# Loading q and k in 1 KB runs with a GpSimd re-layout, and a new set of order offsets, in a threshold-attention and SwiGLU kernel

## The chip, the core and the metric

The kernel runs on one core of a Trainium2 chip. The core has five engines that run side by side and meet only at semaphores: TensorE (PE, with its weight loads shown apart as PEld), VectorE (DVE), ScalarE (ACT), GpSimd (POOL) and SyncE (SP). SP does no arithmetic here; it issues transfers to the core's 16 DMA engines. Each engine works through its own queue strictly in order: an instruction that waits holds everything behind it on that engine.

The metric is the device time of one execution in microseconds (us), median of several runs.

## What is computed

Two stages. The first is an attention in which only scores within `tau` of their row's maximum count; the second is a normalised SwiGLU feed-forward layer on its result.

```python
# q, k, v: (8 batches, 8 heads, 576, 64) f32; tau = 0.02
scores = scale * (q @ k.T)
thresh = max(scores, axis=-1) - tau
scores = where(scores >= thresh, scores, -1e9)
attn = softmax(scores)
x = (attn @ v) -> (4608 tokens, 512)

# x: (4608, 512); w_gate, w_val: (512, 1536); w_out: (1536, 512)
xn = x / sqrt(mean(x * x) + 1e-6) * rms_g
out = (silu(xn @ w_gate) * (xn @ w_val)) @ w_out
```

## The kernel before, in words

**Tiling.** A batch has 576 rows: 512 main rows and 64 tail rows. The main rows are cut into four chunks of 128 (row `4*si + sc` belongs to chunk `sc`), and the tails of two batches make one more chunk, so there are 36 chunks. A step is one chunk with one pair of heads, so there are 4 steps in a chunk and 144 steps in all.

**A step.** PE multiplies q with k into the PSUM tiles `s_ps` (`emit_burst`, L604). DVE copies the scores out, negated and scaled, with a running row minimum `mx` (L637). POOL makes the bias `nth = mx + tau` from it (L678), a tiny instruction. ACT then masks and exponentiates: in the first 16 steps both heads of a pair go through ACT alone (two L689 and one L696); later one head goes through ACT (L689, L693) and the other through an exponential on ACT (L708) with a mask and a product on POOL (L722, L727). The result `wsb` is transposed, in the first 16 steps by PE (L741) and DVE copies (L750), later by a DMA transpose that SP issues (L756). PE multiplies it with v (`emit_av`, L774 and L779), DVE divides by the row sum (L796, L797), and for each chunk ACT and POOL normalise it (L814 to L822) and SP issues another DMA transpose into `xnT` (L826).

**The feed-forward layer** takes 4 chunks at a time (2 in the first two groups). For each of 12 slices of the hidden width PE makes the gate (L880) and the value (L885), ACT a tanh (L894), DVE two products (L897, L902) into `hf`; then PE multiplies with `w_out` (L951; L926 in the last group, which is streamed), a copy goes to `osb` and SP or ACT issues the store.

**Loads of q and k** (`emit_qk`, L310): for each later batch (1 to 7) and each of 4 pairs of heads there are two loads, k and q, of 256 KB. The destination `qkn` has, in one partition, the order chunk, head, element. In HBM one partition's four rows lie together for one head (4 x 64 floats, 1 KB), so the load is cut into runs of one row (64 floats, 256 B). Three `qkn` buffers take turns (`NQK = 3`); a load into one waits on SP until PE has transposed what was in it (L329). The 16 transposes put q and k of a pair into PSUM, and DVE and ACT copy them to `qkt` (L342, L340). Batch 0 has its own loads (`emit_first`): `load_k` L370 and `load_q` L380, into the same `qkn` buffers.

**v and the weights.** v is loaded in runs of 1 KB into the staging buffers `vst` (L524), from which POOL casts it to f16 in the layout that PE wants (L512). The gate and value weights come through three staging buffers (L1016) and are scaled and cast by POOL (L1023), two casts a load; a load waits on SP until the casts of the load three before it are done. `w_out` is loaded and cast by POOL's own DMA queue (L1035).

**Order.** Nothing is ordered by hand. Every piece of work is an `Op` with an engine, a planned cost, a priority (mostly its step number) and dependencies. `order_ops` plays the engines forward with the planned costs; on each engine it picks, among what can start soonest, the smallest priority. `RANK` adds a constant to the priority of each kind of work, by the function that emits it and the inner function that does it. The order that comes out is the fixed order of each engine's queue. On PE the scores of steps from 32 on come in bursts of 1024 columns, 1.78 steps.

Of the kernel before, what the change touches and what calls it, by code (L numbers as in the profile page):

```python
# [11 lines left out]
ALU = mybir.AluOpType  # L12

LAT = dict(PE=200.0, ACT=130.0, DVE=175.0, POOL=20.0, SP=0.0)
SELF = dict(PE=0.0, ACT=125.0, DVE=178.0, POOL=0.0, SP=0.0)
COST = dict(
    s_main=965.0, s_virt=960.0, tr_qk=570.0, tr4=230.0, tr_full=440.0, av_main=300.0, av_virt=370.0, ffn4=215.8, warm=3500.0,
    evac_qk=600.0, evac_qk_act=465.0, evac_half=252.0, evac_kt=330.0, evac_kt_act=252.0, prelu=667.0, exp2=1060.0, exp1=666.0, exp0=590.0,
    mask_d=680.0, mask_g=1810.0, take_g=1360.0, trw=510.0, evac_w=400.0, evac_wp=900.0, rz=210.0, xmul=341.0, sq=612.0, xn=773.0,
    pool_tiny=302.0, pool_mean=944.0, pool_dma=880.0, cast_v=620.0, cast_vt=475.0, cast_w=665.0,  # L20
    sp=420.0, sp_v=600.0, sp_w=600.0, sp_tr=1300.0, sp_qk=680.0, sp_tl=630.0,
)
DMA_NS = dict(qk=1250.0, tl=700.0, v=880.0, vt=350.0, wt=1700.0, xt=800.0, out=800.0, w=820.0, wo=2500.0)
SWITCH = 125.0

RANK = dict(
    ACT={"emit_ffn/ev": 110, "emit_ffn/store": -50, "emit_ffn/tanh": -20, "emit_k_tail/ev": 100, "emit_q_tail/ev": 60, "emit_qk/ev": -40,
        "emit_softmax/ex": 10, "emit_softmax/prelu": 60, "emit_x/sq": -10, "load_k/load": -80, "transposed/ev": 20},
    DVE={"emit_av/half": -120, "emit_burst/ttr": 31, "emit_ffn/ev": 250, "emit_ffn/gate": 90, "emit_ffn/silu": 29, "emit_k_tail/ev": 30, "emit_qk/ev":
        90, "emit_softmax/ev": 180, "setup/<lambda>": -90, "setup/consts": -110, "setup/vconst": 140, "transposed/ev": 80},  # L30
    PE={"emit_av/fn": 1, "emit_burst/fn": -1.1, "emit_ffn/gmm": 5.1, "emit_ffn/omm": 4.4, "emit_ffn/vmm": 0.7, "emit_k_tail/tr": 30, "emit_q_tail/tr":
        -50, "emit_qk/tr": -90, "emit_softmax/tr": -140, "setup/warm": -10, "transposed/tr": -50},
    POOL={"emit_softmax/mask": -60, "emit_softmax/nthr": -20, "emit_softmax/take": -20, "emit_x/mean": -120, "emit_x/norm": -120, "round_/<lambda>":
        -80, "setup/<lambda>": 70, "main/<lambda>": 60},
    SP={"emit_ffn/store": 50, "emit_qk/load": 110, "emit_softmax/tdma": -180, "emit_tail_load/load": 70, "emit_v/load": 17, "emit_v/load_tail": 60,
        "emit_x/tr": 80, "load_k/load": -10, "load_kt/<lambda>": -40, "load_q/load": 50, "load_q0/<lambda>": -60, "setup/<lambda>": 30, "main/load":
        17},
)


# [109 lines left out]
def kernel(  # L150
# [12 lines left out]
    nc = tc.nc  # L163
    B, H, S, D = q.shape
# [5 lines left out]
    MAIN = 512  # L170
# [6 lines left out]
    def sb(name, shape, dt=FP32):  # L177
        return konst.tile(shape, dt, tag=name, name=name)
# [10 lines left out]
    wv = [sb(f"wv{d}", [128, DFF], FP16) for d in range(4)]  # L189
    wo = sb("wo", [128, NFC, DM], FP16)  # L190
    qkn = [sb(f"qkn{i}", [128, 2, 4, 2, D]) for i in range(NQK)]
    qtl = [sb(f"qtl{i}", [128, H, D]) for i in range(2)]
    ktl = [sb(f"ktl{i}", [128, H, D]) for i in range(2)]

# [47 lines left out]
    def gated(o, step):  # L242
        gates.append((o, step))
        return o

    def add(eng, cost, prio, deps, fn, **kw):
        o = Op(eng, cost, prio, deps, fn, **kw)
        ops.append(o)
        return o
# [11 lines left out]
    for s, (ci, p) in enumerate(steps):  # L261
        kind, b, _ = chunks[ci]
        if kind == "m":
            first_step.setdefault(b, s)
        else:
            v_step.setdefault(b, s)

    last_s = {}
    last_sv = {}
    last_av = {}  # L270
# [39 lines left out]
    def emit_qk(b, p, prio):  # L310
        dst = qkT[b % 2][p]
        n = len(tr_of[0])
        nat = qkn[n % NQK]
        los = []
        for j, src in ((1, k), (0, q)):
            before = [tr_of[j][n - NQK]] if n >= NQK else []

            def load(o, j=j, src=src):
                nc.sync.dma_start(out=nat[:, j], in_=src[b, 2 * p:2 * p + 2, 0:MAIN].rearrange(
                    "h (si sc) d -> si sc h d", sc=4))  # L320

            los.append(gated(add("SP", COST["sp_qk"], prio - 3, before, load, dma=DMA_NS["qk"], bulk=True), prio - 3))

        def tr(o):
            for j in (1, 0):
                for c in range(4):
                    for r, rs in enumerate(HALF):
                        at = 256 * j + 64 * c
                        nc.tensor.transpose(ring[o.slot[r]][:, at:at + 64],  # L329
                                            nat[rs, j, c].rearrange("s h d -> s (h d)"), id32[rs, rs])  # L330


        t = gated(add("PE", COST["tr_qk"], -500.0, los + [o_id] + last_s.get(("k", b - 2, p), []), tr, ring="R",
                      nring=2, mode=1), prio)
        done = []
        for r, rs in enumerate(HALF):
            def ev(o, r=r, rs=rs):
                src = ring[t.slot[r]].rearrange("p (j c n) -> p j c n", j=2, n=64)
                if EVAC[r] == "ACT":
                    nc.scalar.copy(out=dst[:, :, :, rs], in_=src)  # L340
                else:
                    nc.vector.tensor_copy(out=dst[:, :, :, rs], in_=src)  # L342

            done.append(add(EVAC[r], COST["evac_qk" if EVAC[r] == "DVE" else "evac_qk_act"], prio, [t], ev, frees=(t, r)))
        for j in range(2):
            tr_of[j].append(t)
        for c in range(4):
            qk_ready[b, p, c] = done

    def emit_first():  # L350
# [13 lines left out]
        def load_k(p, prio):  # L364
# [6 lines left out]

            return add("SP" if p else "ACT", COST["sp_qk"], prio, before, load, dma=DMA_NS["qk"], bulk=True)

# [10 lines left out]
        def transposed(load, srcs, dsts, prio, engines):  # L384
# [9 lines left out]
            for e, (eng, lo, hi) in enumerate(engines):  # L394
                def ev(o, eng=eng, lo=lo, hi=hi):
                    copy = nc.scalar.copy if eng == "ACT" else nc.vector.tensor_copy
                    for i, m, dst in dsts:
# [16 lines left out]
        def emit_k(p, load, prio):  # L414
            nat = qkn[p % NQK]
            t, k_ready[p] = transposed(load, [pair(nat[:, 1, c]) for c in range(4)],
                                       [(0, 2, qkT[0][p][:, 1, 0:2]), (2, 2, qkT[0][p][:, 1, 2:4])], prio,
                                       [("ACT" if p in (1, 2) else "DVE", 0, 2), ("ACT", 2, 4)])
            tr_of[1].append(t)
# [589 lines left out]
    for c in range(DFF // 512):  # L1009
        for d in range(0, 4, 2):  # L1010
            for w_dram, w_sb in ((moe_w_gate, wg), (moe_w_val, wv)):
# [7 lines left out]
                lo = gated(add("SP", COST["sp_w"], pr, w_use[slot], load, dma=2 * DMA_NS['w'], bulk=True), pr)  # L1019
# [14 lines left out]
    for j in range(4):  # L1034
        o = add("POOL", COST["pool_dma"], W_FROM + W_STEP * n + j + WO_AT, [], lambda o, j=j: nc.gpsimd.dma_start(  # L1035
            out=wo[:, 3 * j:3 * j + 3], in_=wo_src[:, 3 * j:3 * j + 3]), dma=DMA_NS['wo'], bulk=True)
# [4 lines left out]
    for s, (ci, p) in enumerate(steps):  # L1041
        kind, b, c = chunks[ci]
# [5 lines left out]
        if p == NP - 1:  # L1048
            gi, j = place[ci]
# [65 lines left out]
HALF_PRIO = 1.2  # L1115
WAYS = ("pg", "pp")
NSTAGE = 3
NQK = 3
W_FROM = 2.0
W_STEP = 0.4  # L1120
N_XPE = 0
# [41 lines left out]
```

## Time and profile before

| | |
|---|---|
| median of 3 runs | 550.42 us (550.23 to 550.43) |
| time of the profiled execution | 550.23 us |
| its span, first to last instruction | 548.5 us |
| granted TensorE clock | 0.999 |
| PE / PEld busy | 535.6 / 296.4 us |
| DVE / ACT / POOL busy | 452.5 / 432.8 / 322.0 us |
| DMA packets | 270,023, of them 252,544 under 512 B; 89.04 MB |

The page gives, for each engine, the time in which it was busy, then the span in 40 equal slices (each digit is a share in tenths), and groups of instructions by line: shapes, count, busy us and mean ns of one, then the idle time of the engine just before them with what ended it. An arrow `<-` between tiles reads "written from"; after an idle time it reads "released by". In a view in order of time the first number is the start in us, the second the duration, and a bracket gives the idle time before. A busy PE is not PE at its peak, since matmuls are pipelined and their ends are modelled.

### The profile page before, as it was taken

Reading aid. Unit: us, or ns where it says so; the run is one execution under the profiler, and the core shown is the slowest. Engines: PE = TensorE matmul, PEld = TensorE weight load, DVE = VectorE, ACT = ScalarE, POOL = GpSimd, SP = SyncE. Lnnn points to the kernel's source line nnn. Section 1 sums busy time; section 2 is a strip of 40 time slices with the busy share of each in tenths; the row PEclk is TensorE's granted clock in tenths of the full one; section 3 lists DMA queues with packets and bytes.
Section 4 is the critical chain, followed back from the end, with each engine's and each line's share of the span. In section 5 each row is a group of like instructions: output and inputs, shape, how many; then the busy total and the mean of one; then the engine's idle time right before and its main releaser. Section 6 shows DMA issues by size and latency. Waiting matters only on the chain.

```text
span 548.5 us, 14654 instructions
## 1 busy us (share of the span) xinstructions
PE 535.6 (98%) x5444; PEld 296.4 (54%) x5444; DVE 452.5 (83%) x1300; ACT 432.8 (79%) x684; POOL 322.0 (59%) x462
## 2 busy tenths in 40 slices
PE   8899999999999999999999999999999999999996
PEld 4566766664655464546554565556555454544442
DVE  4899988878998799979988888888988788875643
ACT  5799998978898798978988988888889787882211
POOL 1567947784767667666776775667657664641000
PEclk9999999999999999999999999999999999999999
DMA  9999999969998899789998999789987758562102
GB/s 192 259 266 287 181 166 211 182 134 213 165 173 138 190 163 188 164 188 167 188 190 137 165 175 216 176 145 194 209 171 117 119 94 127 114 128 51 39 20 96
DMA packets 270023, 89.04 MB, mean 162 GB/s; under 512 B 252544, under 2 KB 262272, under 8 KB 269952
## 3 DMA queue, kind: packets, MB, share of 16 engines
q1 hardware_dynamic: 267024, 85.76, 81.9%
q0 software_dynamic: 1600, 1.57, 1.9%
q8 instruction: 42, 0.69, 0.6%
q10 hardware_dynamic: 1328, 0.79, 0.5%
q14 instruction: 29, 0.24, 0.2%
HBM read 37.75 MB, written 9.44 MB: 86 GB/s over the span
## 4 chain that ended last, share of the span: by engine, by line
PE 78%; DMA 7%; DVE 7%; ACT 2%; POOL 2%; issue 2%; SPq 2%; DVEq 0%; POOLq 0%; ACTq 0%
PE s_ps L604 23%; PE ring L880 14%; PE ring L951 14%; PE ring L885 13%; PE ring L779 5%; DVE ssb L637 3%; PE ring L329 2%; DMA qkn<-in_q_dram 2%; PE ring L774 2%; PE s_ps L926 2%; DMA vst<-in_v_dram 2%; DMA stg<-in_moe_w_val_dram 1%; DMA stg<-in_moe_w_gate_dram 1%; PE s_ps L885 1%; DVE sl L897 1%
## 5 line engine op out<-in xcount | busy, mean ns | idle before, releaser
L689 ACT ACTIVATE ssb<-ssb,nth 128x576 f32<-128x576 f32 x224 | 165.7, 765 | 24.3 <-POOL nth L678 24.0
L637 DVE CUSTOM_DVE_ANT_0 ssb<-s_ps,zrow 128x576 f32<-128x576 f32 (+8 forms) x288 | 172.8, 635 | 12.4 <-PE s_ps L604 10.9
L604 PE MATMUL s_ps<-qkt 64*64 64x288 f32 (+17 forms) x1660 | 154.0, 414 | 0.8 <-ACT ssb L689 0.4
L722 POOL TENSOR_SCALAR wsb<-ssb,nth 128x576 f16<-128x576 f32 x64 | 110.5, 1727 | 8.4 <-DMA wt<-wsb 4.2
L604 PEld LDWEIGHTS s_ps<-qkt 64*64 64x64 f32 (+1 forms) x1660 | 78.2, 145 | 56.2 <-issue 23.4
L880 PE MATMUL ring<-xnT,wg 128*128 128x512 f16 (+1 forms) x456 | 107.0, 357 | 0.0
L885 PE MATMUL ring<-xnT,wv 128*128 128x512 f16 (+1 forms) x448 | 104.8, 356 | 0.0
L696 ACT ACTIVATE wsb<-ssb 128x1152 f16<-128x1152 f32 x80 | 92.7, 1159 | 1.2
L894 ACT ACTIVATE th<-ring 128x512 f32<-128x512 f32 (+1 forms) x114 | 61.4, 540 | 39.2 <-PE ring L880 39.1
L678 POOL TENSOR_SCALAR nth<-mx 128x2 f32<-128x2 f32 x144 | 31.6, 220 | 101.3 <-DVE mx L637 87.9
L727 POOL TENSOR_TENSOR wsb<-wsb,esb 128x576 f16<-128x576 f16 x64 | 81.8, 1279 | 5.8 <-ACT esb L708 1.4
L897 DVE SCALAR_TENSOR_TENSOR sl<-th,ring 128x512 f32<-128x512 f32 (+1 forms) x114 | 71.2, 625 | 15.0 <-ACT th L894 14.0
L637 DVE CUSTOM_DVE_ANT_0 ssb<-s_ps,zrow,mxp 128x128 f32<-128x128 f32 (+7 forms) x112 | 53.5, 515 | 30.4 <-PE s_ps L604 29.6
L885 PEld LDWEIGHTS <-wv 128*128 128x128 f16 x480 | 45.7, 98 | 47.2 <-issue 3.8
L880 PEld LDWEIGHTS <-wg 128*128 128x128 f16 x480 | 42.6, 98 | 43.4 <-issue 6.8
L708 ACT ACTIVATE esb<-ssb,nth 128x576 f16<-128x576 f32 x64 | 49.2, 769 | 16.0 <-POOL nth L678 15.7
L779 PE MATMUL ring<-va,wt 128*128 128x65 f16 (+1 forms) x1264 | 50.2, 193 | 0.0
L779 PEld LDWEIGHTS <-wt 128*128 128x128 f16 (+1 forms) x1280 | 46.1, 100 | 3.5 <-issue 0.8
L951 PE MATMUL ring<-wo,hf 128*128 128x512 f16 x204 | 47.7, 379 | 0.0
L693 ACT ACTIVATE wsb<-ssb 128x576 f16<-128x576 f32 x64 | 43.5, 679 | 1.3
L951 PE MATMUL ring<-wo,stg 128*128 128x512 f16 x168 | 39.2, 379 | 0.0
L902 DVE TENSOR_TENSOR stg<-ring,sl 128x512 f16<-128x512 f32 (+1 forms) x56 | 35.1, 631 | 3.8 <-DVE sl L897 0.5
(76 smaller groups left out, 569.7 us busy)
## 6 DMA issues: line engine op xcount, KB each, us to landing
vst<-in_v_dram SPq DMA_DIRECT2D x32, 256.0 KB, 3.5
qkn<-in_k_dram SPq DMA_DIRECT2D x31, 256.0 KB, 4.1
out_dram<-osb SPq DMA_DIRECT2D x29, 256.0 KB, 2.9
qkn<-in_q_dram SPq DMA_DIRECT2D x28, 256.0 KB, 4.5
stg<-in_moe_w_gate_dram SPq DMA_DIRECT2D x6, 512.0 KB, 6.9
stg<-in_moe_w_val_dram SPq DMA_DIRECT2D x6, 512.0 KB, 7.0
wt<-wsb SPq DMA_TRANSPOSE x128, 3.8
wo<-in_moe_w_out_dram POOLq DMA_DIRECT2D x4, 384.0 KB, 7.9
```

Source lines behind the costliest of these rows:

```text
L604: nc.tensor.matmul(s_ps[h][rows, at:at + hi - lo], lhs(hs), kT[i][p][h][hs, lo:hi], start=True, stop=True)
L637: nc.vector.tensor_tensor_reduce(out=ssb_of(s)[:, h, lo:hi], in0=s_ps[h][:, at:at + hi - lo], in1=zrow[:, lo:hi], scale=-1.0 / 8.0, scalar ...
L689: nc.scalar.activation(out=sb_[:, h], in_=sb_[:, h], func=PRELU, scale=-1.0, bias=nth[m][:, h:h + 1], **PRELU_KW)
L696: nc.scalar.activation(out=wsb[s % NW], in_=sb_, func=AF.Exp)
L722: nc.gpsimd.tensor_scalar(out=wsb[s % NW][:, h], in0=sb_[:, h], scalar1=nth[m][:, h:h + 1], scalar2=None, op0=ALU.is_le)
L727: nc.gpsimd.tensor_tensor(out=wsb[s % NW][:, h], in0=wsb[s % NW][:, h], in1=esb[es], op=ALU.mult)
L779: nc.tensor.matmul(ring[o.slot[0]][rs, at:at + D + 1], w[:, 5 * h + j, rs], va[vi][:, p, 2 * j + h], start=False, stop=(h == 1 and j == 3))
L880: nc.tensor.matmul(ring[o.slot[0]][:, 0:n], wg[d][:, fs], xnT[slot][:, d, 0:n], start=(d == 0), stop=(d == 3))
L885: nc.tensor.matmul(ring[o.slot[0]][:, 0:n], wv[d][:, fs], xnT[slot][:, d, 0:n], start=(d == 0), stop=(d == 3))
L894: nc.scalar.activation(out=th[i][:, 0:n], in_=ring[g.slot[0]][:, 0:n], func=AF.Tanh, scale=0.5)
L897: nc.vector.scalar_tensor_tensor(out=sl[i][:, 0:n], in0=th[i][:, 0:n], scalar=1.0, in1=ring[g.slot[0]][:, 0:n], op0=ALU.add, op1=ALU.mult)
L951: nc.tensor.matmul(ring[(first or o).slot[0]], hf[hs[fc][0]][:, 128 * j:128 * (j + 1)], wo[:, fc], start=(fc == 0), stop=(fc == NFC - 1))
```

## The change

Three things change.

1. `emit_qk` loads k and q into new staging buffers `qst` (two of them, each 128 x 2 x 4 x 64 floats) in runs of 1 KB, as v is loaded. A new POOL instruction, `mix`, copies a `qst` buffer into `qkn` in the order that PE's transposes want. The load waits for the last mix of its buffer; the mix waits for its load and for PE's transposes of what was in `qkn`; PE's transposes wait for the mix.
2. `qkn` has two buffers instead of three (`NQK = 2`). This holds for the loads of batch 0 too.
3. `RANK` has other offsets for nearly every kind of work on every engine.

In the changed kernel `qst` is loaded at L324 and mixed at L328; lines up to 191 keep their number, later ones move by 1, from 268 by 2, and from 323 by 12.

```diff
 RANK = dict(
-    ACT={"emit_ffn/ev": 110, "emit_ffn/store": -50, "emit_ffn/tanh": -20, "emit_k_tail/ev": 100, "emit_q_tail/ev": 60, "emit_qk/ev": -40,
-        "emit_softmax/ex": 10, "emit_softmax/prelu": 60, "emit_x/sq": -10, "load_k/load": -80, "transposed/ev": 20},
-    DVE={"emit_av/half": -120, "emit_burst/ttr": 31, "emit_ffn/ev": 250, "emit_ffn/gate": 90, "emit_ffn/silu": 29, "emit_k_tail/ev": 30, "emit_qk/ev":
-        90, "emit_softmax/ev": 180, "setup/<lambda>": -90, "setup/consts": -110, "setup/vconst": 140, "transposed/ev": 80},
-    PE={"emit_av/fn": 1, "emit_burst/fn": -1.1, "emit_ffn/gmm": 5.1, "emit_ffn/omm": 4.4, "emit_ffn/vmm": 0.7, "emit_k_tail/tr": 30, "emit_q_tail/tr":
-        -50, "emit_qk/tr": -90, "emit_softmax/tr": -140, "setup/warm": -10, "transposed/tr": -50},
-    POOL={"emit_softmax/mask": -60, "emit_softmax/nthr": -20, "emit_softmax/take": -20, "emit_x/mean": -120, "emit_x/norm": -120, "round_/<lambda>":
-        -80, "setup/<lambda>": 70, "main/<lambda>": 60},
-    SP={"emit_ffn/store": 50, "emit_qk/load": 110, "emit_softmax/tdma": -180, "emit_tail_load/load": 70, "emit_v/load": 17, "emit_v/load_tail": 60,
-        "emit_x/tr": 80, "load_k/load": -10, "load_kt/<lambda>": -40, "load_q/load": 50, "load_q0/<lambda>": -60, "setup/<lambda>": 30, "main/load":
-        17},
+    ACT={"emit_ffn/ev": -30, "emit_ffn/store": -10, "emit_ffn/tanh": -140, "emit_k_tail/ev": -130, "emit_q_tail/ev": 30, "emit_qk/ev": -200,
+        "emit_softmax/ex": 270, "emit_softmax/ex2": 140, "emit_softmax/prelu": 90, "emit_x/sq": 10, "load_k/load": -210, "transposed/ev": 20},
+    DVE={"emit_av/half": -30, "emit_burst/ttr": -19, "emit_ffn/ev": -180, "emit_ffn/gate": 120, "emit_ffn/silu": -17.6, "emit_k_tail/ev": -210,
+        "emit_softmax/ev": 40, "setup/<lambda>": -40, "setup/consts": 60, "setup/vconst": -60, "transposed/ev": 30},
+    PE={"emit_av/fn": -79, "emit_burst/fn": -220, "emit_ffn/gmm": -84, "emit_ffn/omm": 160, "emit_ffn/vmm": 147, "emit_k_tail/tr": -90,
+        "emit_q_tail/tr": -120, "emit_qk/tr": 160, "emit_softmax/tr": 40, "setup/warm": -20, "transposed/tr": 60},
+    POOL={"emit_qk/mix": 10, "emit_softmax/mask": 140, "emit_softmax/nthr": -30, "emit_x/mean": 10, "emit_x/norm": -290, "round_/<lambda>": 60,
+        "setup/<lambda>": -60, "main/<lambda>": 50, "main/cast": 50},
+    SP={"emit_ffn/store": 90, "emit_qk/load": 140, "emit_softmax/tdma": -70, "emit_tail_load/load": 50, "emit_v/load": 40, "emit_v/load_tail": -10,
+        "emit_x/tr": -170, "load_k/load": -40, "load_kt/<lambda>": -50, "load_q/load": -40, "load_q0/<lambda>": -120, "setup/<lambda>": 10,
+        "main/load": -80},
 )
...
     qkn = [sb(f"qkn{i}", [128, 2, 4, 2, D]) for i in range(NQK)]
+    qst = [sb(f"qst{i}", [128, 2, 4, D]) for i in range(NQS)]
...
+    qst_use = []
...
             before = [tr_of[j][n - NQK]] if n >= NQK else []
 
-            def load(o, j=j, src=src):
-                nc.sync.dma_start(out=nat[:, j], in_=src[b, 2 * p:2 * p + 2, 0:MAIN].rearrange(
-                    "h (si sc) d -> si sc h d", sc=4))
+            ns = len(qst_use)
+            raw = qst[ns % len(qst)]
 
-            los.append(gated(add("SP", COST["sp_qk"], prio - 3, before, load, dma=DMA_NS["qk"], bulk=True), prio - 3))
+            def load(o, j=j, src=src, raw=raw):
+                nc.sync.dma_start(out=raw.rearrange("s h c d -> s h (c d)"),
+                                  in_=src[b, 2 * p:2 * p + 2, 0:MAIN].rearrange("h (si sc) d -> si h (sc d)", sc=4))
+
+            def mix(o, j=j, raw=raw):
+                nc.gpsimd.tensor_scalar(out=nat[:, j].rearrange("s c h d -> s h c d"), in0=raw, scalar1=1.0, scalar2=1.0,
+                                        op0=ALU.mult, op1=ALU.mult)
+
+            lo = gated(add("SP", COST["sp_v"], prio - 3, qst_use[ns - len(qst):ns - len(qst) + 1] if ns >= len(qst) else [], load, dma=DMA_NS["v"], bulk=True), prio - 3)
+            mi = add("POOL", COST["cast_v"] + MIX, prio - 1, [lo] + before, mix)
+            qst_use.append(mi)
+            los.append(mi)
...
-NQK = 3
+NQK = 2
+NQS = 2
+MIX = 50.0
```

## The prediction

> **What bounds the kernel now.** I read the page first, then the busy times by window, then the waits, then the first 20 us in order of time. The page's engine row, its slices of PE and DMA, and the chain:
>
> ```profile
> PE 535.6 (98%) x5444; PEld 296.4 (54%) x5444; DVE 452.5 (83%) x1300; ACT 432.8 (79%) x684; POOL 322.0 (59%) x462
> ...
> PE   8899999999999999999999999999999999999996
> ...
> DMA  9999999969998899789998999789987758562102
> ...
> PE 78%; DMA 7%; DVE 7%; ACT 2%; POOL 2%; issue 2%; SPq 2%; DVEq 0%; POOLq 0%; ACTq 0%
> ```
>
> TensorE sets the time: it is short of full only in the first two slices and the last. The transfers are full at the start. Windows (us, then PE, PEld, DVE, ACT, POOL busy with counts, clock, DMA share, GB/s):
>
> ```profile
> 0.00:60.00 60.00, 53.38 (x651) 33.98 (x652) 47.11 (x136) 49.95 (x76) 34.03 (x71) 1.00 1.10 245
> 60.00:120.00 60.00, 59.89 (x775) 39.88 (x777) 52.04 (x152) 53.12 (x96) 43.21 (x59) 1.00 1.02 175
> 120.00:470.00 350.00, 348.43 (x3574) 187.92 (x3566) 306.91 (x918) 299.68 (x466) 230.17 (x313) 1.00 0.90 166
> 470.00:548.00 78.00, 73.86 (x458) 34.63 (x454) 46.45 (x95) 30.09 (x49) 14.63 (x21) 1.00 0.32 74
> ```
>
> From 60 to 470 us PE is idle 1.7 us; in the first 60 it is idle 6.6. So the change can gain only in the first 60 us, in small stalls later and in the tail, while every us that it takes from PE anywhere is paid in full. I also took the time from each PE block's first matmul to the next block's and fitted it by shape (216 ns for 512 fp16 columns, 110 for 256, 91 ns to enter 64-row tiles from full ones, 272 ns to leave them). The fit adds to 531.0 us; the blocks took 543.0. The 12.0 us between are the stalls: 6.9 before 60 us, 3.2 between 120 and 210, 1.3 up to 500, 0.7 after. The rest of the span is 1.2 us before the first matmul and 4.2 after the last began to drain.
>
> Why the start stalls shows in POOL's and ACT's order of time:
>
> ```profile
> 14.80 0.41 POOL L512 TENSOR_SCALAR va<-vtl 64x256 f16<-64x256 f32 x1 [0.21 <-DMA vtl<-in_v_dram]
> 17.82 0.63 POOL L512 TENSOR_SCALAR va<-vst 128x512 f16<-128x512 f32 x1 [2.60 <-DMA vst<-in_v_dram]
> 18.52 0.51 POOL L678 TENSOR_SCALAR nth<-mx 128x2 f32<-128x2 f32 x2
> ...
> 18.77 1.44 ACT L689 ACTIVATE ssb<-ssb,nth 128x576 f32<-128x576 f32 x2 [2.78 <-POOL nth L678]
> ```
>
> A cast that waits for its load holds the tiny nth (L678) behind it, and ACT's softmax waits for nth: 2.8 us here. From 18.77 to 59 us ACT is back to back, some 2.55 us a step (1.44 for two L689, the rest L696), and PE has no other work yet. ACT bounds the first 60 us, and POOL's queue decides whether ACT gets holes. Rows for POOL and loads:
>
> ```profile
> L722 POOL TENSOR_SCALAR wsb<-ssb,nth 128x576 f16<-128x576 f32 x64 | 110.5, 1727 | 8.4 <-DMA wt<-wsb 4.2
> L727 POOL TENSOR_TENSOR wsb<-wsb,esb 128x576 f16<-128x576 f16 x64 | 81.8, 1279 | 5.8 <-ACT esb L708 1.4
> L512 POOL TENSOR_SCALAR va<-vst 128x512 f16<-128x512 f32 x32 | 20.0, 626 | 23.1 <-DMA vst<-in_v_dram 22.7
> ...
> vst<-in_v_dram SPq DMA_DIRECT2D x32, 256.0 KB, 3.5
> qkn<-in_k_dram SPq DMA_DIRECT2D x31, 256.0 KB, 4.1
> qkn<-in_q_dram SPq DMA_DIRECT2D x28, 256.0 KB, 4.5
> ```
>
> **The loads.** 56 loads (batches 1 to 7) go from 1024 packets of 256 B to 256 of 1 KB. In the trace a 256 B packet took 23.8 ns in the mean, a 1 KB one 64.9. So (4 x 23.8 - 64.9) x 14,336 packets / 16 engines = 27 us of the sixteen engines' time go, some 5% of the span, about 5 us of it in the first 60. A qst load should land like vst (3.5 us; 4.8 in the first 60 us) and not like qkn (4.1 to 4.5; 6.0 to 6.7 there). After 60 us PE's one long stall, 1.6 us near 129, is of this kind: k and q were issued at 123.8 and 124.5 and landed 5.7 and 5.8 us later, the moments at which PE's two halves of the transposes began. So after 60 us faster loads alone are worth some 2 us.
>
> **The mixes.** 56 new POOL instructions, 128x512 f32 to f32, which no row has. Lower bound L512's 626 ns, same form with an f16 result; upper bound L722's 1727 x 512/576 = 1535 ns; the other rows of this form (L822, L1023) have 690 to 694. Taken: 650, being nearest to L512: 56 x 0.65 = 36.4 us, POOL 322 to 358. The cover is POOL's idle 41%; where it is missing, nth is late, then L689 and L708 on ACT, then the P transposes on SP's queue, then the AV matmuls. By the order of the changed kernel POOL has 22.1 us of work between step 16 and 24 (before: 16.8) against 25.0 us of PE work: 88%.
>
> GpSimd is warned against for this: the Trainium skill, "GPSIMD Engine Reference", section "Elementwise — side-by-side cycle accounting", gives some 769 ns for 512 elements at best, which would make an estimate of 43 us where L512's row makes 35. Its section "Specifications" says that GpSimd shares its SBUF interfaces with VectorE and that some DVE forms contend; here L897 has a mean of 681 ns from 150 to 400 us, with POOL at 68%, and 686 after 512 us with POOL idle, so the trace shows no contention, and by it the mixes cost DVE nothing.
>
> **PE's own work.** The same matmuls in another order. Priced by the fit the new order makes 531.9 us: one switch more each way (0.36) and other places for the score blocks in 64 or 128 rows (0.55). **+0.9.**
>
> **Order and waits, first 60 us.** With two qkn buffers instead of three, k of pair 2 and 3 and q of pair 2 and 3 of batch 0 wait for PE's transposes; behind them on SP stand the v loads, the first qst and the weights. I followed the new queues by hand with SP's issues from the rows (0.6 us), landings of 4.4 (k, q), 4.8 (v, qst) and 6.9 us (weights, L1016), L1023 0.69 and the ACT times above. The second score block waits for q of pair 1 in PE's order (+0.6). But nth of step 2 no longer stands behind a late cast: step 3 of the softmax starts near 20.3 (before: 21.32), and step 10 near 41.0 (41.61). Then POOL catches up with ACT: its order puts mixes, four weight casts and wo's issue (0.88) between the nths. Two weight loads wait on SP for stage buffers whose casts are now later, and the tenth (issued near 41.9) lands near 48.9; its casts stand before nth of step 13, which comes near 50.5 with ACT free at 50.0. Step 13 near 50.7 (before: 49.88), step 16 near 60.3 (59.34). **+1.0**; with weights landing in 5.3 us (the least in the trace) +0.3, in 8.3 (the most) +2.5. PE has nothing to fill that time with.
>
> **Steps 16 to 32.** The new order places 2.2 us less FFN work before step 32 (98.4 us of PE work against 100.6), so attention must run faster, with POOL at 80 to 88%. Bounds 0 and 2.2; ACT is idle 6.9 us of 60 there; taken **+0.7**.
>
> **From step 32 on.** By step numbers (one step is some 3.3 us of PE) a load stands 2 to 5 steps ahead of its mix on POOL, and the mix 2 to 5 ahead of PE's transposes. A qst load waits on SP for the last mix of its buffer, and the P transposes queue behind it; that mix stands beside the nth of at most one step later, and nth is ahead of the same step's transpose by the whole softmax, so as a rule no new wait opens. Near 129 us k's load stands one transpose earlier than now and q's where it was, with a mix more to go. The PE work between a step's scores and its AV matmul covers the whole softmax; from step 16 on its least is 10.1 us before and 10.3 after, its median 13.5 in both. The stalls of 4.4 us between 120 and 500 can go (-4.4) or double (+4.4); POOL's longer queue makes it **+0.5**.
>
> **Tail.** Before, the last group's output matmuls stand between its gate and value matmuls, and PE stalls 0.5 near 519 for a gate product. In the new order the 84 last matmuls are all output ones, with their factors long made: **-0.5**. The final copies and store are as before.
>
> **Sum.** 0.9 + 1.0 + 0.7 + 0.5 - 0.5 = +2.6 on the span of 548.5: 551.1. The profiled execution's time lies 1.8 us above its span (550.23), and the median 0.2 above that (550.42): **553.0 us**, 0.5% slower. A difference under 0.2% (1.1 us) can't be told from none.
>
> **Rivals.** *Faster:* lighter transfers keep POOL's casts from waiting. The hole of 2.8 us goes and none comes back, the stall of 1.6 us near 129 us goes, the tail gives 0.5 and PE's order takes 0.9: -4.0, 546.4. For it: casts wait 22.7 us for v loads now. Against: 56 more casts that can wait likewise. It decides at step 13: nth before 49.9. Chance 0.29. *No change:* the first 60 us even out (0), 0.9 - 0.5 stay: 550.8. Chance 0.18. *POOL becomes the bound:* a mix costs like the two-operand L727 (1279). Six mixes between steps 10 and 16 add 6 x 0.63 = 3.8, and steps 16 to 24 get 22.1 + 5 x 0.63 = 25.3 against 25.0 of PE, say 1.2 with late nths: 558. Against: L512 has one operand, and so has the mix. Chance 0.13. *The forecast:* 551.6 to 555.5. Chance 0.40. *The loads don't change in kind* (packets stay at 270,023): excluded by their access patterns, and within the second case if not.
>
> **The numbers.** Slower 0.40 + 0.13 = 0.53, same 0.18, faster 0.29. The range for 8 in 10 leaves out the far ends of the first and third rival: 546 to 559.
>
> **What would show it.** Packets near 227,000 with 195,000 under 512 B; POOL near 358 us with 56 instructions of 630 to 700 ns; qst landing near 3.5 us; ACT's first L689 of step 13 after 50 us and a wait of L689 for nth before 60 us; PE idle 7 to 9 us in the first 60 us. I am wrong if PE's idle before 60 us falls under 5, if a mix takes over 1 us, or if PE is idle over 6 us between 120 and 470.

## The result, and the profile after

| | before | after |
|---|---|---|
| median | 550.33 us (550.01 to 550.43, 4 runs) | 553.3 us (551.77 to 554.3, 4 runs) |
| ratio, 95% interval | | 1.0053 (1.0028 to 1.0078) |
| profiled execution: time, span | 550.23, 548.5 us | 551.77, 550.0 us |
| PE blocks by the fit; what they took | 531.0; 543.0 us | 531.9; 544.6 us |

The change costs 3.0 us. The profiled execution is the fastest of after's four, 1.5 us under the median; where the others lose that is a question of its own below. Its page (engines; slices of PE and DMA; packets; the mix's group; landings):

```profile
PE 534.8 (97%) x5432; PEld 294.8 (54%) x5432; DVE 451.2 (82%) x1300; ACT 428.4 (78%) x684; POOL 355.3 (65%) x518
...
PE   7899999999999999999999999999999999999896
...
DMA  8997998998978989989995898988985487631013
...
DMA packets 227016, 89.05 MB, mean 162 GB/s; under 512 B 195200, under 2 KB 219264, under 8 KB 226944
...
L328 POOL TENSOR_SCALAR qkn<-qst 128x512 f32<-128x512 f32 x56 | 34.1, 618 | 15.1 <-DMA qst<-in_k_dram 8.9
...
qst<-in_k_dram SPq DMA_DIRECT2D x28, 256.0 KB, 3.9
qst<-in_q_dram SPq DMA_DIRECT2D x28, 256.0 KB, 3.8
stg<-in_moe_w_gate_dram SPq DMA_DIRECT2D x6, 512.0 KB, 5.6
stg<-in_moe_w_val_dram SPq DMA_DIRECT2D x6, 512.0 KB, 4.7
```

Read the PE row at both ends. The first slice is a 7 where it was an 8, though over the first 60 us PE is idle as long as before (6.5 and 6.6 us, windows below). Near the end there is an 8 that was not there: PE isn't full some 30 us before the span ends. The transfers are lighter (the DMA row has fewer 9s), a mix takes 618 ns, and the weights land in 5.6 and 4.7 us where they took some 7 before. The windows give the size of it (columns as before the change):

```profile
0.00:60.00 60.00, 53.46 (x661) 35.49 (x665) 48.06 (x140) 51.32 (x81) 39.75 (x81) 1.00 0.96 252
60.00:120.00 60.00, 60.00 (x782) 39.30 (x780) 53.72 (x161) 52.71 (x94) 50.10 (x70) 1.00 0.98 176
120.00:470.00 350.00, 349.60 (x3582) 187.07 (x3584) 307.51 (x922) 299.55 (x471) 254.56 (x354) 1.00 0.85 166
470.00:549.00 79.00, 71.70 (x420) 32.96 (x412) 41.89 (x80) 24.82 (x41) 10.90 (x16) 1.00 0.28 68
```

From 60 to 470 us PE is idle 0.4 us (before: 1.7), though POOL is busy 50.1 of the 60 us up to 120 (before: 43.2). The loss stands in the last window: 7.3 of 79 us not busy, against 4.1 of 78.

To set runs side by side I use the prediction's fit of PE's blocks by shape: a kernel's own order is priced with it, and what its blocks took beyond that price is called its stalls. One unit is a window of one profiled execution:

| stalls, us | 0 to 60 | 60 to 120 | 120 to 470 | after 470 |
|---|---|---|---|---|
| before | 6.9 | 0.0 | 4.4 | 0.6 |
| after | 5.9 | -0.4 | 2.4 | 4.8 |

So in this execution the change won 3.4 us of stalls before 470 us, lost 4.2 after, and PE's own order costs 0.9.

The early stall, in POOL's and then ACT's order of time:

```profile
19.89 0.62 POOL L328 TENSOR_SCALAR qkn<-qst 128x512 f32<-128x512 f32 x1 [4.30 <-DMA qst<-in_k_dram]
20.59 0.21 POOL L690 TENSOR_SCALAR nth<-mx 128x2 f32<-128x2 f32 x1
```

```profile
20.84 1.44 ACT L701 ACTIVATE ssb<-ssb,nth 128x576 f32<-128x576 f32 x2 [1.44 <-POOL nth L690]
...
49.08 1.43 ACT L701 ACTIVATE ssb<-ssb,nth 128x576 f32<-128x576 f32 x2
```

The first mix now does what the cast of v did before: it waits for its load with nth behind it. ACT loses 1.4 us instead of 2.8. The softmax of step 13 starts at 49.08 without a wait, 0.8 us earlier than before; the prediction had 50.7.

The tail, on PE, on DVE and on ACT (L892 gate, L897 value, L963 output matmuls, L906 tanh, L909 and L914 DVE's two products):

```profile
493.93 1.46 PE L963 MATMUL s_ps<-wo,stg 128*128 128x512 f16 x6 [0.78 <-DVE hf L914]
...
501.69 1.03 PE L892 MATMUL s_ps<-xnT,wg 128*128 128x512 f16 x4
502.56 1.03 PE L897 MATMUL s_ps<-xnT,wv 128*128 128x512 f16 x4
503.42 1.03 PE L892 MATMUL s_ps<-xnT,wg 128*128 128x512 f16 x4
...
506.37 1.02 PE L892 MATMUL s_ps<-xnT,wg 128*128 128x512 f16 x4 [1.06 <-DVE sl L909]
...
513.84 1.02 PE L897 MATMUL s_ps<-xnT,wv 128*128 128x512 f16 x4 [1.26 <-DVE stg L914]
...
521.04 1.02 PE L892 MATMUL s_ps<-xnT,wg 128*128 128x512 f16 x4 [1.00 <-DVE sl L909]
```

```profile
493.18 0.69 DVE L914 TENSOR_TENSOR hf<-s_ps,sl 128x512 f16<-128x512 f32 x1 [0.71 <-PE s_ps L963]
...
505.64 0.68 DVE L909 SCALAR_TENSOR_TENSOR sl<-th,s_ps 128x512 f32<-128x512 f32 x1
...
513.09 0.69 DVE L914 TENSOR_TENSOR stg<-s_ps,sl 128x512 f16<-128x512 f32 x1
...
520.31 0.68 DVE L909 SCALAR_TENSOR_TENSOR sl<-th,s_ps 128x512 f32<-128x512 f32 x1
```

```profile
503.68 0.60 ACT L906 ACTIVATE th<-s_ps 128x512 f32<-128x512 f32 x1 [8.50 <-PE s_ps L897]
```

Eleven gate and value pairs follow one another with no output matmul between them. Each takes two of the eight PSUM slots, which tanh and DVE's two products free. Four slots are the halves of the two `s_ps` tiles: in the plan that `order_ops` makes, slots 4 and 5 are one tile, 6 and 7 the other.

At 506.37 the third gate goes into slot 7. That slot's last user had left it at 496.11; what PE waits for is DVE's product on slot 6, the other half of the tile (505.64, over at 506.32). At 513.84 and 521.04 it is the same: slot 7 had been free for some 5 us, and PE starts when the product on slot 6 is over (513.78 and 520.99). Before 493.93 it goes both ways: DVE's product on slot 6 waited 0.71 us for output matmuls in slot 7, and the next output matmuls needed that product. By the times between PE's blocks these four stalls are 0.9, 1.2, 1.4 and 1.2 us, all that is lost after 470 us.

The tanh shows the same thing: the first gate's matmuls were followed by the value's at 502.56, yet its tanh starts only at 503.68, when the value's matmuls (next block at 503.42) are over. Gate and value stand in slots 4 and 5 there. The semaphores in the trace say that the program waits: the gate's four matmuls raise none, the value's last one (503.20) raises the one that the tanh waits for. The gate at 503.42, whose value stands in another tile, raises its own, and its tanh starts at 504.53, 0.25 us after the gate.

### The profile page after: what moved, and what is told of

Same layout as the page of the kernel before. It is cut to its first block, busy times and chain, and to the rows that moved or that the text cites. A ratio compares the mean times of both kernels' runs of the same rounds, so it can differ in the third digit from the quotient of the medians.

```text
span 550.0 us, 14718 instructions
## 1 busy us (share of the span) xinstructions
PE 534.8 (97%) x5432; PEld 294.8 (54%) x5432; DVE 451.2 (82%) x1300; ACT 428.4 (78%) x684; POOL 355.3 (65%) x518
## 2 busy tenths in 40 slices
DMA packets 227016, 89.05 MB, mean 162 GB/s; under 512 B 195200, under 2 KB 219264, under 8 KB 226944
## 4 chain that ended last, share of the span: by engine, by line
PE 86%; ACT 6%; DVE 4%; DMA 1%; SPq 1%; issue 1%; POOL 0%; DVEq 0%; ACTq 0%; POOLq 0%
PE s_ps L616 26%; PE ring L892 15%; PE ring L963 15%; PE ring L897 15%; PE ring L791 6%; ACT ssb L701 3%; PE ring L341 2%; PE ring L786 2%; ACT wsb L708 2%; PE s_ps L938 2%; DVE ssb L649 2%; PE s_ps L897 2%; PE s_ps L892 1%; DVE stg L914 1%; DMA qst<-in_k_dram 1%; DVE sl L909 1%
## 5 line engine op out<-in xcount | busy, mean ns | idle before, releaser
L701 ACT ACTIVATE ssb<-ssb,nth 128x576 f32<-128x576 f32 x224 | 165.6, 767 | 39.3 <-POOL nth L690 38.8
L616 PE MATMUL s_ps<-qkt 64*64 64x288 f32 (+15 forms) x1648 | 153.3, 414 | 1.2 <-ACT qkt L412 0.7
L616 PEld LDWEIGHTS s_ps<-qkt 64*64 64x64 f32 (+1 forms) x1648 | 76.9, 145 | 57.8 <-issue 21.8
L897 PE MATMUL ring<-xnT,wv 128*128 128x512 f16 (+1 forms) x436 | 101.8, 356 | 0.6 <-ACT qkt L352 0.5
L892 PE MATMUL ring<-xnT,wg 128*128 128x512 f16 (+1 forms) x436 | 102.1, 357 | 0.2 <-DVE xsb L809 0.2
L708 ACT ACTIVATE wsb<-ssb 128x1152 f16<-128x1152 f32 x80 | 92.8, 1160 | 1.4
L892 PEld LDWEIGHTS <-wg 128*128 128x128 f16 x480 | 43.5, 98 | 56.0 <-issue 16.6
L909 DVE SCALAR_TENSOR_TENSOR sl<-th,ring 128x512 f32<-128x512 f32 (+1 forms) x109 | 67.5, 622 | 5.8 <-ACT th L906 5.6
L906 ACT ACTIVATE th<-ring 128x512 f32<-128x512 f32 (+1 forms) x109 | 58.5, 539 | 14.0 <-PE ring L892 13.2
L897 PEld LDWEIGHTS <-wv 128*128 128x128 f16 x480 | 43.0, 98 | 41.9 <-issue 5.6
L963 PE MATMUL ring<-wo,hf 128*128 128x512 f16 x216 | 49.8, 379 | 0.0
L328 POOL TENSOR_SCALAR qkn<-qst 128x512 f32<-128x512 f32 x56 | 34.1, 618 | 15.1 <-DMA qst<-in_k_dram 8.9
L976 DVE TENSOR_SCALAR osb<-ring 128x512 f32<-128x512 f32 x31 | 21.3, 688 | 21.3 <-PE ring L963 18.6
```

The costliest lines, as they stand in the source:

```text
L616: nc.tensor.matmul(s_ps[h][rows, at:at + hi - lo], lhs(hs), kT[i][p][h][hs, lo:hi], start=True, stop=True)
L701: nc.scalar.activation(out=sb_[:, h], in_=sb_[:, h], func=PRELU, scale=-1.0, bias=nth[m][:, h:h + 1], **PRELU_KW)
L708: nc.scalar.activation(out=wsb[s % NW], in_=sb_, func=AF.Exp)
L892: nc.tensor.matmul(ring[o.slot[0]][:, 0:n], wg[d][:, fs], xnT[slot][:, d, 0:n], start=(d == 0), stop=(d == 3))
L897: nc.tensor.matmul(ring[o.slot[0]][:, 0:n], wv[d][:, fs], xnT[slot][:, d, 0:n], start=(d == 0), stop=(d == 3))
L906: nc.scalar.activation(out=th[i][:, 0:n], in_=ring[g.slot[0]][:, 0:n], func=AF.Tanh, scale=0.5)
```

## The experiments

Twelve kernels ran, in groups on one chip each with the kernel before beside them. Its medians there were 551.08, 549.72, 550.80 and 550.74, with single executions from 548.21 to 553.95, so it scatters as the changed kernel does; a kernel is compared by its ratio to the runs beside it.

| | median us | ratio to before, 95% | stalls 0-60, 60-120, 120-470, after 470 |
|---|---|---|---|
| e1 the changed kernel | 552.65 | 1.0033 (1.0017, 1.0050) | 5.5, -0.9, 3.5, 4.8 |
| e2 old FFN offsets in three groups | 566.13 | 1.0271 (1.0243, 1.0300) | 6.3, -0.8, 12.8, 9.5 |
| e3 loads, old offsets | 562.46 | 1.0215 (1.0190, 1.0240) | 9.4, 3.4, 9.2, 0.6 |
| e4 offsets, old loads | 556.76 | 1.0104 (1.0075, 1.0133) | 6.7, 0.6, 6.3, 2.0 |
| e5 tail spread | 550.48 | 1.0010 (0.9992, 1.0029) | 8.3, -0.1, 2.3, 2.6 |
| e6 mixes twice | 569.99 | 1.0368 (1.0346, 1.0390) | 11.8, 2.2, 12.4, 5.0 |
| e7 runs of 256 B | 560.39 | 1.0200 (1.0171, 1.0230) | 8.1, 2.9, 4.7, 5.0 |
| e8 before with copies | 554.19 | 1.0097 (1.0069, 1.0125) | 8.4, 1.3, 5.1, 0.6 |
| e9 mixes cut | 551.32 | 1.0014 (0.9997, 1.0031) | 6.0, -1.3, 2.1, 4.8 |
| e10 tail, two late | 550.02 | 0.9989 (0.9971, 1.0006) | 5.9, -0.2, 2.3, 1.8 |
| e11 the same, q mixes on DVE | 555.42 | 1.0088 (1.0064, 1.0112) | 6.7, -0.5, 7.5, 1.8 |
| e12 the same as e10, slots apart | 549.26 | 0.9975 (0.9958, 0.9992) | 7.0, -0.4, 3.6, 2.0 |

**e1, the changed kernel again.**

> The changed kernel as it is, to see where its slower executions lose their 1 to 2.5 us against the fastest (551.8). By the tail theory (the loss stands after 470 us, where the new offsets put the output matmuls behind all gate and value matmuls, +4.2 us there, and all before 470 us is gained or even) the stalls after 470 us are again 4.5 to 5.1 us in this profile, whatever its time, and the median is 553.3 within 0.8. By the mix theory (POOL's 34 us of mixes make nth late here and there) a slower profile has its extra time before 470 us, in waits of ACT for nth or of PE for transposes.

The tail's stalls are 4.8 us again, to the hundredth. What moves from execution to execution is early, or as here near 126 us, in POOL's order of time:

```profile
126.66 0.62 POOL L328 TENSOR_SCALAR qkn<-qst 128x512 f32<-128x512 f32 x1 [3.31 <-DMA qst<-in_q_dram]
```

SP issued that load of q at 120.67, 0.5 us earlier than in the other profile (121.21), but it landed some 5.9 us later instead of 4.0, and PE's transposes waited 1.4 us for the mix. So the loss after 470 us is the same in both profiles, and one load that lands late can cost 1.4 us. Where the slower executions lose their time stays open: this profile is one of the fast ones, 0.2 us above the first.

**e2, the offsets of before for gate, value and output matmuls, in the last three groups.**

```diff
-            o.prio += RANK[o.eng].get(...)
+            o.prio += TAIL_RANK[kind] if o.tail and kind in TAIL_RANK else RANK[o.eng].get(...)
+TAIL_FROM = 24
+TAIL_RANK = dict(gmm=5.1, vmm=0.7, omm=4.4)
```

> The changed kernel with the three offsets of before for gate, value and output matmuls (5.1, 0.7, 4.4) in the last three groups alone; PE's order is the same up to some 430 us, and output matmuls then stand between the gate and value matmuls. PE's matmuls by the fit: 531.6 us against 531.9. Tail theory: stalls after 470 us fall from 4.8 to 0.5 to 1.2, the median falls by 4.0 to 549.3 (548.3 to 550.5). Mix theory, or a loss spread over the span: the median stays at 552.3 to 554.

A miss, 13 us slower. The feed-forward work of these groups came forward, and the last score blocks were left with nothing between them: near 464 and 469 us a score block waited 2.3 and 2.5 us for DVE's copy of the one before. The granted clock fell as well: 0.68 from 470 to 475 us and 0.66 to 480, where it is 1.00 in the changed kernel, and output matmuls followed one another every 0.43 us up to 480 us and every 0.22 after it. The run says nothing on the tail; it says that an offset given to three groups moves work 40 us away from where one looks.

**e3 and e4, each half of the change alone.** e3 is the changed kernel with before's whole `RANK`, e4 is before with the new one.

> The 1 KB loads, the mixes and two qkn buffers with every order offset of before. Tail theory: the tail is as before (0.7 us of stalls), and what the changed kernel won before 470 us (some 3.5 us of stalls) belongs to the loads: 547 (545.5 to 548.5). Mix theory: POOL's mixes make the same late nth here: 552 to 555. If what was won before 470 us came from the offsets and not from the loads: 550 to 551.

> The loads of before (256 B runs straight into three qkn buffers, no mix) with the new offsets. Tail theory: the tail costs 4.2 us, PE's order 0.8, nothing is won earlier: 555.4 (553.5 to 557). Mix theory: without mixes the loss is gone: 549.5 to 551.

Each half alone costs more than both: +11.4 and +5.7 us against +1.6 on the same chip. e3's tail is as good as before's (0.6), so the tail's loss needs the new offsets; but the loads with the old offsets cost 2.5 us in the first 60, 3.4 in the next and 4.8 to 470. My tail theory had 547 here and is wrong on this half. The new offsets aren't an extra beside the loads: without them the loads lose.

e4 settles something about the tail. It has the new offsets, and its tail's stalls are 2.0 us, not 4.8. Twelve gate and value pairs stand in a row there, from 506.05 to 526.76, with no output matmul between them (L880 gate, L885 value, L951 output, L964 copy):

```profile
506.05 1.03 PE L880 MATMUL s_ps<-xnT,wg 128*128 128x512 f16 x4
...
526.76 4.05 PE L951 MATMUL s_ps<-wo,hf 128*128 128x512 f16 x18
531.60 1.46 PE L951 MATMUL s_ps<-wo,hf 128*128 128x512 f16 x6 [0.78 <-DVE osb L964]
```

The 24 blocks take 20.7 us, 0.86 each, as PE makes them without a stall. So pairs without output matmuls between them needn't stall. In e4's plan all eight slots go round; in the changed kernel's an output sum that is begun at 500.40 and finished at 526.65 holds one of them, and the other seven come in an order in which PE writes slot 7 while slot 6 is still read. e4's two stalls (502.16 and 531.60) are PE waiting for the copy of the other half.

**e6, e9 and e8: what POOL's time costs.** e6 issues every mix twice and e9 cuts each to one chunk of four, both in the changed kernel's order. e8 keeps before's order on every engine and adds 56 copies that nobody waits for:

```diff
+                if b:
+                    nc.gpsimd.tensor_scalar(out=spare, in0=spare, scalar1=1.0, scalar2=1.0, op0=ALU.mult, op1=ALU.mult)
                 src = ring[t.slot[r]].rearrange("p (j c n) -> p j c n", j=2, n=64)
```

> The changed kernel with every mix issued twice, in the same order (the planner isn't told): POOL 355 to 390 us. POOL theory (what the loads alone lost, 11.4 us in the run before, is POOL's 34 us of mixes, a third of each us): 560 to 564. Order theory (those 11.4 us come from the reshuffled order that the old offsets give with the new operations, and POOL's slack takes the mixes themselves): 552.7 to 555.7.

> The changed kernel in its own order, each mix cut to the first of its four chunks (it leaves out three quarters of the copy, so later chunks are computed from stale q and k). POOL has some 23 us less to do. If POOL's time costs as in the doubled mixes (half a us for each us, as POOL is at its limit already): 541 (539 to 543). If the price falls off below the limit, to the 0.15 us for each us that the copies in the kernel before showed: 549.2 (548 to 550.5). If the mixes as they are cost nothing: 552 to 553.3.

> The kernel before, in its own order on every engine, with 56 POOL copies of 128x464 f16 that nobody waits for, two behind each set of q and k transposes (some 0.56 us each, 31 us in all). POOL theory: 8 to 11 us slower, 559 to 562. Order theory: 0 to 3 us slower, 551 to 554.

A straight line doesn't fit. The cut mixes took 298 ns, 18 us less in all, and gained about 1 us, which the overlapping intervals (e1's and e9's) don't tell from nothing. The doubled ones took 34.7 us more and cost 17 to 18. The copies in the kernel before (580 ns each, 32.5 us) cost 4.5 (5.3 by the ratio). So the last 18 us of the mixes cost about 1 us in this order, and another 34 us on top of them cost half their length. What the first 16 cost no run shows. In e6 the waits show the way it goes (total us, times, longest):

```profile
ACT ssb L703 <- POOL nth L692: 65.9, 56, 2.8
...
PEld ring L343 <- POOL qkn L330: 4.6, 6, 1.3
```

ACT waits 65.9 us for nth (38.8 in the changed kernel; before, 24.0 at L689 and 15.7 at L708). The second mixes make nth late; the transposes hardly wait for the mixes themselves.

**e7, runs of 256 B in the changed kernel.** The load writes the order chunk, head, element into `qst`, and the mix copies straight (621 ns). Order and instructions are the same.

```diff
-                nc.sync.dma_start(out=raw.rearrange("s h c d -> s h (c d)"),
-                                  in_=src[b, 2 * p:2 * p + 2, 0:MAIN].rearrange("h (si sc) d -> si h (sc d)", sc=4))
+                nc.sync.dma_start(out=raw.rearrange("s h c d -> s (h c d)").rearrange("s (c h d) -> s c h d", c=4, h=2),
+                                  in_=src[b, 2 * p:2 * p + 2, 0:MAIN].rearrange("h (si sc) d -> si sc h d", sc=4))
```

> The changed kernel with k and q brought into the staging buffers in runs of 256 B, already in the order chunk, head, element, and a mix that copies straight; same order on every engine. Packets 270,000 again. If the 1 KB runs are what wins time before 470 us (weights landing in 4.7 to 5.6 us instead of 6.9, no long stall near 126): 555 to 557. If packets don't matter on the path: 552 to 553.5.

8 to 9 us slower than the changed kernel (7.7 by the medians, 9.2 by the ratios), more than either theory had. Its waits:

```profile
ACT ssb L701 <- POOL nth L690: 47.0, 41, 2.5
POOL qkn L328 <- DMA qst<-in_k_dram: 12.6, 11, 4.1
POOL qkn L328 <- DMA qst<-in_q_dram: 6.7, 7, 2.2
```

POOL waits 19.3 us for q and k (12.9 in the changed kernel) and ACT 8.2 us more for nth. The median landings of k and q hardly differ (4.2 and 4.0 us; the changed kernel 3.9 and 3.8, e1 4.0 and 4.1), so it is single late loads that POOL waits for. That its queue hands them on to ACT fits these waits; it was not tested by itself.

**e5, the tail's output matmuls spread.** Once the last attention matmul is placed, the seven pieces of six output matmuls that are left of the last group but one go one behind each pair:

```diff
-                opts.append((t, o.prio, i))
+                opts.append((t, o.prio if heads or o.tail is None else o.tail, i))
...
+            g.tail, vv.tail = 10.0 * fc, 10.0 * fc + 1.0
...
+                    o.tail = 10.0 * len(outs) + TAIL_O if parts[0][0] >= 28 else -1.0
...
+                mo.tail = 10.0 * (fc + OUT_LAG) + 8.0
```

> The changed kernel, with the same order on PE up to matmul 4310 of 4480 (the 42 output matmuls that end near 501.7 us); after that the seven remaining pieces of six output matmuls of the last group but one stand one behind each gate and value pair instead of behind all of them. Tail theory: stalls after 470 us fall from 4.8 to 0.5 to 1.2, all before is as it was: 548.6 (547.6 to 549.8). If the stalls of the tail only move, into the products of the last pairs or the final copies: 551.5 to 553.

Stalls after 470 us fell from 4.8 to 2.6 and the end from 4.2 to 3.6 us: 2.8 won there. The median fell by 2.2 (1.3 by the ratios). What is left by the trace is 0.9 at 496.62, 0.75 at 509.89 and some 0.9 at 544.62, where PE waits for ACT's copy of the sum in the other half of its tile (543.97 to 544.57), and not, as the expectation of e10 has it, for the last gate product. The rest of the gain is hidden by this profile's first 60 us, though its order there is the changed kernel's:

```profile
25.00 1.37 POOL L1041 TENSOR_SCALAR wg<-stg,rmsg 128x512 f16<-128x512 f32 x2 [2.35 <-DMA stg<-in_moe_w_gate_dram]
```

The cast of the first weights waited 2.35 us for its load, where it waited 0.20 in the changed kernel's first profile and 0.42 in e1; the first 60 us have 8.3 us of stalls instead of 5.5 to 5.9, and step 13 starts at 51.33 instead of 49.08.

**e10 and e11: two pieces kept for the end; then the q mixes on DVE.**

> As the run with the seven pieces spread, but five of them behind the first five pairs and two behind the last pair, so that the last group's output matmuls needn't wait for the last gate product (1.0 us near 540 there). Tail theory: stalls after 470 us 1.5 to 1.9, the median 549.5 (548.6 to 550.3). If the two late pieces delay the final copies and the store instead: 550.3 to 551.2.

> The same with the 28 mixes of q put on VectorE, at the same place in the order, the 28 of k left on POOL: POOL has 17 us less to do, DVE some 10 to 19 us more of its 452. If POOL's time is what the mixes cost: 2 to 4 us below the run with POOL doing both, 546.5 (545.5 to 547.5). If DVE, at 85 to 89% between 60 and 470 us, has no more room than POOL: equal or slower, 549.5 to 555.

e10: that last stall is gone (1.8 us after 470), the time 550.02, level with before. e11: DVE does a mix in 604 ns in the mean, 16.9 us in all, POOL has 14.7 us less, and the time is 5.4 us longer than e10, nearly all of it between 120 and 470 us. So for these mixes DVE, at 88 to 89% from 60 to 470 us in e10, has less room than POOL. The mean hides something (least, median and most ns of one mix on DVE):

```profile
L331 DVE TENSOR_SCALAR qkn<-qst x28: 416/509/1322, 27.4 to 400.4; 128x512 f32<-128x512 f32 x28
```

The five DVE mixes beside which POOL had nothing to do took 418 to 422 ns. Beside POOL's mask (L737) most took 669 to 829, and the longest ran beside POOL's product (L742). POOL's own mixes took 612 to 622 all along. So DVE's copy is held up by POOL here, some 5 us over the 28; how much of the 5.4 us that makes is open.

**e12, the slots apart.** In the tail a slot in one half of an `s_ps` tile is taken only if the other half is free or no other slot is:

```diff
-                got = min(f for f in ring_free[o.ring] if o.pick is None or f[1] in o.pick)
+                idle = {f[1] for f in ring_free[o.ring] if f[0] <= t}
+                got = min((f for f in ring_free[o.ring] if o.pick is None or f[1] in o.pick),
+                          key=lambda f: (f[0] > t, not heads and f[1] >= 4 and f[1] ^ 1 not in idle, f))
```

> As the run with five pieces spread and two at the end, but in the tail a PSUM slot in one half of an s_ps tile is taken only if the other half is free, or no other slot is. In the trace of the changed kernel a tanh whose gate stood in one half started only when the value matmuls in the other half had ended (503.68, gate's end 502.56, value's end 503.42), and a gate product in one half waited for output matmuls in the other (493.42). Sharing theory: the stalls of 0.93 near 491.9 and 0.75 near 505.8 go, stalls after 470 us 0 to 0.4, the median 548.4 (547.5 to 549.2). If the waits are for the slot's own earlier user: no change, 549.5 to 550.5.

e10's two stalls, which ended at 494.17 and 507.44, are gone, as the sharing theory says, and the first pair's tanh starts 0.26 us after its gate again. New ones, 2.0 us together, stand in the last block of output matmuls:

```profile
541.84 1.89 PE L944 MATMUL s_ps<-wo,stg 128*128 128x512 f16 x8 [0.78 <-DVE osb L984]
544.50 0.81 PE L944 MATMUL s_ps<-wo,stg 128*128 128x512 f16 x3 [0.78 <-DVE ssb L984]
```

It is the same thing once more: the new rule handed the last group's four sums their slots in the order 4, 6, 5, 7, so that parts that follow one another share a tile, and PE waits for the copy of the part before. Still the kernel is at 549.26, 0.25% under before (0.08 to 0.42) and some 3.3 us under the changed kernel. Other slots for the four sums should take these away too; that was not run.

## Why the prediction was right, and where it was not

The forecast was 553.0 us with +2.6 on the span; the median is 553.3, and by e1's ratio 552.2. The mechanism it named as the likeliest (slower by a little, no engine newly the bound) holds. Its terms do so only in part.

- **Packets, mixes, POOL.** 227,016 packets, 195,200 of them short, POOL 355 us, a mix 618 ns: as worked out. The Trainium skill, "GPSIMD Engine Reference", section "Elementwise — side-by-side cycle accounting", gives 769 ns; L512's row was the better guide, though as a lower bound its 626 was a little high. Its section "Specifications" names contention for DVE instructions with two SBUF inputs or in a 2-port mode. L897, from which the prediction read that there is none, has one of its inputs in PSUM and couldn't show it. For the work that DVE has in this kernel the reading holds: in e6, with 390.9 us of POOL, DVE's busy time is 452.3 us against 451.2. But DVE's mixes in e11 do show contention, 418 to 422 ns alone and up to 1322 beside POOL.
- **PE's order, +0.9.** It goes into every run's stalls as the fit has it; no run measured it by itself.
- **First 60 us, +1.0: the wrong sign in the profile.** After has 1.0 us less than before, e1 1.4 less, e5 1.4 more, e10 1.0 less, e12 0.1 more, all with one order there, so the term is smaller than the scatter of one order. The step that failed is the hole before step 13. The prediction had 9.7 us from step 10 to step 13, with nth behind the casts of a weight load that lands after 6.9 us, as in the trace before; these five profiles have 8.4 to 8.6 (before: 8.3). Step 13 came at 49.08 and not at 50.7. The weights landed in 4.7 to 6.3 us there, but with short packets too they took 5.4 to 6.1 (e4, e7): that lighter neighbours made them faster isn't shown. That a late weight makes this term positive is right (e5).
- **Steps 16 to 32, +0.7: the wrong sign.** 60 to 120 us gained 0.4. POOL at 50.1 of 60 us was carried: by e9 the mixes' last 18 us are worth about 1 us over the whole run.
- **From step 32 on, +0.5: the wrong sign, within its bounds.** -2.0 (e1: -0.9). The stall near 129 us shrank to 0.3 when the loads landed in time; in e1, when one did not, it was 1.9.
- **Tail, -0.5: the wrong sign and the largest miss, +4.2.** The step read "the 84 last matmuls are all output ones, with their factors long made". That is so, and it looked at the wrong matmuls: it put at nothing what the new order does to the slots of the pairs before them. There PE waits four times, 4.8 us in all, for work on the other half of an `s_ps` tile. e12 takes two such stalls, 1.7 us, away by its slots; e5, e10 and e12 give back 2.8, 3.1 and 3.4 us (stalls and the end together), with output matmuls spread among the pairs as well. That the pairs need those as cover isn't shown: e4's twelve pairs have none and don't stall.
- **The rival of POOL as the bound** put a doubled mix at 558. e6 has it at 570.0: six mixes before step 16 and five after it were counted, but not that every later nth goes late as well.

So the sum came out because two errors cancel, and that is luck. The tail is 4.7 us worse than its term. What stands before 470 us is better than its three terms (+2.2) by 5.6 us in the profile, and by 4.3 in the median (3.0 - 0.9 - 4.2 = -2.1). What e3 loses by its old offsets is not settled between the reshuffled order, the two `qkn` buffers and the waits of the mixes; e8's copies, at other places in POOL's queue, suggest some 4.5 of its 11.4 us for POOL's time. Of the signs that the prediction named, packets, POOL and landings came; step 13 after 50 us and PE idle 7 to 9 us in the first 60 did not (49.08; 6.5).

## What to carry to other kernels

Price work on an engine off the path from both sides of its slack: 18 us less of it gained about 1 us here, 35 us more cost 17, in one and the same order. When matmuls are moved, look at the buffers of what stays behind, not only at where they go: here another rotation of the same slots made PE wait for the other half of a tile whose own half was free. New operations and new order offsets have to be judged together, since the halves of this change alone cost 11.4 and 5.7 us and both together 1.6 on the same chip.

## What was unexpected

- Runs of 1 KB are worth 8 to 9 us in the changed kernel's order, where the transfers' busy share gave no hint of more than 2.
- Two PSUM slots that are halves of one tile wait for one another in this program. A tanh on one half started at 503.68, after the matmuls in the other half (502.56 to 503.42), and in e12 PE waited 0.78 us twice for DVE's copy of the other half. These are waits for semaphores, which the program holds; whether the memory would need them, no run here tells.
- The same copy of 128x512 f32 takes 618 to 621 ns on POOL; on DVE it takes 418 to 422 when POOL has nothing to do, and 604 in the mean, as POOL's work beside it holds it up. 128x128 takes POOL 298.
- The kernel before, 0.4 us wide in four runs, was up to 5.5 us wide in groups of 17 to 23 runs. A difference of 1 us between two profiles of different runs is no finding without the runs beside it.
